# Norms of layer 1 made in layer 0, halo copies on Pool's queue, own slots for raw weights: one change to a two-layer attention and feed-forward kernel

## The chip, the cores and the metric

The kernel runs on one NeuronCore of a Trainium2 chip. The metric is device time in microseconds (us) of one execution; lower is better. A core has a matrix engine (PE, with its weight loads shown apart as PEld), a vector engine (DVE), an activation engine (ACT), a general one (POOL) and a sequencer that mostly issues transfers (SP). Each works through its own instructions in a fixed order, and waits on semaphores for the others. Transfers (DMA) are issued by SP, ACT or POOL and carried by 16 DMA engines that they share. In the profile an issue by such a queue is written SPq, ACTq or POOLq.

## The reference, cut to what matters

Two layers with the same weights, over 2048 tokens of width 576:

```python
x = x + _A_ref(_layernorm(x), A_wqkv, A_wo)     # layer 0
x = x + _B_ref(_layernorm(x), B_w1, B_w2)
x = x + _A_ref(_layernorm(x), A_wqkv, A_wo)     # layer 1
x = x + _B_ref(_layernorm(x), B_w1, B_w2)
# _A_ref: 32 heads of 18; each token attends to 8 tokens: itself and those 2, 4, .. 14 before it
# _B_ref: silu(x @ w1) @ w2, hidden width 4608
# _layernorm: (x - mean) / sqrt(var + 1e-5), no gain and no bias
```

## The kernel before

**Tiling.** The tokens are cut into 4 chunks of 512 (4 tiles of 128 tokens, index `j`). With two layers there are 8 stages, `s` = 0 to 7; stage `s` is layer `s // 4`, chunk `s % 4`. Each stage has a norm, the query-key-value product (QKV), the attention, the projection (`project`), a second norm, and the feed-forward part (`ffn`). All products run in f16 pairs: an operand is split into a high and a low half, and a product is the sum of three matmuls. From stage 3 on the first product of `ffn` is made by a scheme with seven products in place of eight (`pair_z`, L1051), whose weights `prepare` makes on DVE, ACT and POOL during layer 0.

**QKV and attention.** Heads are worked in 4 units `u` of 8 heads. For stage 0 and for layer 1 PE makes a unit's QKV for 4 tiles (`qkv_matmul`, L693, 14 matmuls of 432 columns for a tile), and ACT copies keys and values to a tile `kv` (L759) and queries to `qt` (L761). There are two `kv` tiles. A token's older neighbours lie on another partition, so four small transfers copy them within `kv` (`halo`, L771): ACT's queue issues them. Only then can DVE multiply queries by keys (L790, 128x2304 f32), sum (L794), make the softmax, weigh the values (L823) and sum them (L830, L831). For stages 1 to 3 of layer 0 the QKV products are made early, during stage 0, while the raw QKV weights are at hand (`qkv_ahead`; ACT evacuates at L706 and SP stores to DRAM).

**First `ffn`.** During stage 0's `ffn` the weights `w1` and `w2` arrive raw in f32 (`raw_load`, L896 to L900, POOL's queue). ACT sums their squares (L917, L919), PE adds across partitions (L922), DVE makes a power of two (`pow2`), ACT and DVE split into halves (L931 to L938), and POOL's queue stores the halves for later stages (L941, L943). Raw tiles and halves share 8 slots `w1` and 10 slots `w2`.

**Norms.** `layer_norm` takes mean and variance on DVE (L466, L467), an inverse root by three Newton steps of four small DVE instructions each (L490 to L496), then normalizes and splits, on ACT and DVE or on DVE alone, and transposes either on PE (first norm and the stage 0 ones) or by a DMA transpose of SP's queue (L442). Layer 1's first norms are made at the head of stages 4 to 7, on DVE alone (L545, L550, L425).

**What sets the order.** The program is written as operations with a planned engine, duration, priority, reads and writes. A list scheduler (`Plan.order`) plays them through and writes each engine's instructions in the order it finds, lower `prio` first among those ready. `after=` binds the planned order only. On the chip an instruction waits for the data and slots that it uses and for the instructions ahead of it on its engine. So the order of every engine is fixed before the run, and a changed duration or slot moves instructions in places far from the edit.

Of the kernel before, what the change touches and what calls it, by code (L numbers as in the profile page):

```python
# [276 lines left out]
def sliding_attention_silu_ffn(ctx: ExitStack, tc: tile.TileContext, x, wqkv, wo, w1, w2, out):  # L277
# [27 lines left out]
    def cut(a):  # L305
# [49 lines left out]
    xd = [[tc.dram_tile([P, D], F32, name=f"xd{c}{j}") for j in range(NJ)] for c in range(NC)]  # L355
    w1s = [tc.dram_tile([P, 10 * P], F16, name=f"w1s{f}") for f in range(NFT)]
# [37 lines left out]
    d1 = cp.tile([P, NFT], F32, name="d1")  # L394
# [8 lines left out]
    du = cp.tile([P, NU], F32, name="du")  # L403
# [46 lines left out]
    marks = []  # L450

    def layer_norm(xs, prio, into, on_act, on_pe=False, late=()):

        st, mv, nt, xT = Buf("st"), Buf("mv"), Buf("nt"), Buf(into)
# [26 lines left out]
        def newton():  # L481
            v, r, a, b = (T(nt)[:, i, :] for i in (0, 1, 3, 4))
# [6 lines left out]
            for i in range(3):  # L489
                nc.vector.tensor_tensor(a, r, r, op=ALU.mult)  # L490
                nc.vector.tensor_tensor(a, a, v, op=ALU.mult)
                nc.vector.tensor_scalar(b, a, -0.5, 1.5, op0=ALU.mult, op1=ALU.add)
                if i < 2:
                    nc.vector.tensor_tensor(r, r, b, op=ALU.mult)
                else:
                    nc.vector.scalar_tensor_tensor(r, r, LNS, b, op0=ALU.mult, op1=ALU.mult)  # L496
            if on_act == 1:
                nc.vector.tensor_scalar(T(nt)[:, 2, :], T(mv)[:, :, 0], -1.0, None, op0=ALU.mult)
        op("DVE", 2.6, newton, [(st, j) for j in range(NJ)] + [(mv, j) for j in range(NJ) if on_act < 2], [nt], prio)
        if into == "xt":  # L500
            for j in range(2):
# [30 lines left out]
                op("ACT", 2.6, hi, [(ys, 0), (ys, 1)], [(yh, 0)], prio)  # L532
# [7 lines left out]
            return xT  # L540
        for j in range(NJ):
# [10 lines left out]
            if on_act:  # L552
                op("ACT", 0.74, lambda j=j, y=y: nc.scalar.activation(T(y), T(xs[j]), AF.Identity,
                                                                      bias=T(nt)[:, 2, j:j + 1]),
                   [xs[j], nt], [y, (xT, "hold")], prio)
# [31 lines left out]
    def raw_wq(u):  # L587
# [4 lines left out]
        for k in range(5):  # L592
            def load(k=k):
                d = raw(k).rearrange("p (t c) -> p t c", t=3)
                for p0, n, row in ((0, P, k * P),) if k < 4 else ((0, 64, 512), (64, 64, 512)):
                    nc.sync.dma_start(d[p0:p0 + n], wqkv[row:row + n, :].rearrange(
# [4 lines left out]
            op("SP", 0.8 if k < 4 else 1.3, load, [], [rs[k]], WQ[u], nbytes=P * 3 * UC * 4, after=gate[3:4] if u > 1 else ())  # L601
# [6 lines left out]
        def scale():  # L608
# [36 lines left out]
    def raw_wo():  # L645
# [17 lines left out]
        def scale():  # L663
# [6 lines left out]
            nc.vector.tensor_scalar(DO, so[:, 3:4], ru[:, NU:], 1.0 / HSH, op0=ALU.mult, op1=ALU.mult)  # L670
# [19 lines left out]
    def qkv_matmul(xT, w, j, m):  # L690
        pl = list(passes(lambda k: T(xT)[:, k, j * P:(j + 1) * P], w))
# [543 lines left out]
```

## Time and profile before

| | before |
|---|---|
| runs shown | 2209.05, 2196.72, 2195.46 us; median 2196.72 us |
| profiled execution, its own time | 2203.91 us |
| its span, first to last instruction | 2202.1 us |
| PE busy | 2127.9 us, 97% |
| DVE busy | 1649.3 us, 75% |
| ACT busy | 932.9 us, 42% |
| POOL busy | 403.4 us, 18% |

The profiled execution is one run under the hardware profiler; its time is 7.2 us above the median of the runs shown. Shares are means over the whole span, and the stages differ: stage 0 up to its projection lasts to about 195 us, the first `ffn` to about 487 us, layer 1 starts near 975 us. A view by stage says more than the mean. A row of the timeline gives start, duration, engine, line, operation, tiles and count, and in brackets the engine's idle time before it with what ended the wait.

### The profile page before, as it was taken

What the parts mean: (1) busy time and instruction counts of PE and PEld (TensorE: products, weight loads), DVE (VectorE), ACT (ScalarE), POOL (GpSimd) and SP (SyncE); (2) the same over time, 40 slices, a digit from 0 to 9 for tenths busy, and PEclk for the clock granted to TensorE, in tenths of its full rate; (3) what the DMA queues carried; (4) which work ended last, traced back from release to release, by engine and by line L of the source; (5) the groups of instructions that cost most, each with busy time, mean ns of one, the idle gap of its engine ahead of it and who ended that gap; (6) DMA issues with size and microseconds to landing.
All of it is one profiled execution on the core that took longest, in us unless ns stands there. A gap on an engine that the chain in (4) does not pass through costs nothing.

```text
span 2202.1 us, 39553 instructions
## 1 busy us (share of the span) xinstructions
PE 2127.9 (97%) x15676; PEld 1532.1 (70%) x15676; DVE 1649.3 (75%) x2658; ACT 932.9 (42%) x1649; POOL 403.4 (18%) x617
## 2 busy tenths in 40 slices
PE   6799998999999999999999999999999999999999
PEld 3346555666756566577788767887778877888887
DVE  7889899999999985457885479855997559873322
ACT  7245667644243533333432433334443333433332
POOL 2124345421356554400001000000000000000000
PEclk9899999999999999999999999999999999999999
DMA  7777566885787777675556845676655964567542
GB/s 194 147 197 267 182 227 213 206 283 204 198 257 236 242 193 205 206 205 175 174 167 168 242 129 160 176 206 187 194 153 140 263 186 142 162 150 221 156 137 74
DMA packets 295201, 419.64 MB, mean 191 GB/s; under 512 B 150040, under 2 KB 181636, under 8 KB 291048
## 3 DMA queue, kind: packets, MB, share of 16 engines
q1 hardware_dynamic: 249344, 274.91, 45.0%
q0 software_dynamic: 35936, 98.79, 14.1%
q10 hardware_dynamic: 9736, 43.42, 6.2%
q8 instruction: 122, 2.00, 0.4%
q14 instruction: 63, 0.52, 0.1%
HBM read 298.47 MB, written 67.68 MB: 166 GB/s over the span
## 4 chain that ended last, share of the span: by engine, by line
PE 73%; issue 11%; DVE 8%; DMA 6%; ACT 1%; POOL 1%; ACTq 0%; SPq 0%; DVEq 0%; POOLq 0%
PE acc L1137 30%; PE z L1051 17%; PE z L1124 12%; PE z L693 10%; PE acc L862 4%; DMA w<-in_B_w_dram 1%; DVE pr L823 1%; DMA rb<-yh 1%; DVE pr L830 1%; DVE pr L790 1%; DVE lg L794 1%; DVE x L869 1%; DMA qd<-hs 1%; DMA w<-w2s 1%; DVE w L933 1%
## 5 line engine op out<-in xcount | busy, mean ns | idle before, releaser
L1137 PE MATMUL acc<-w,h 128*128 128x288 f16 x6912 | 883.8, 286 | 2.4 <-DVE x L869 2.4
L1137 PEld LDWEIGHTS <-h 128*128 128x128 f16 x6912 | 676.1, 98 | 175.8 <-issue 3.4
L1051 PE MATMUL z<-rb,w 128*128 128x256 f16 (+1 forms) x4410 | 522.5, 273 | 8.5 <-ACT hs L1056 7.5
L1051 PEld LDWEIGHTS <-w 128*128 128x128 f16 (+1 forms) x4410 | 430.1, 98 | 76.4 <-issue 10.5
L1124 PE MATMUL z<-rb,w 128*128 128x512 f16 x1512 | 335.7, 382 | 12.1 <-ACT hs L1126 5.3
L693 PEld LDWEIGHTS <-rb 128*128 128x128 f16 x1792 | 177.3, 99 | 170.9 <-issue 17.2
L869 DVE SCALAR_TENSOR_TENSOR x<-acc,d,x 128x576 f32<-128x576 f32 x192 | 156.2, 815 | 178.3 <-PE acc L1137 177.1
L1124 PEld LDWEIGHTS <-w 128*128 128x128 f16 x1512 | 148.5, 99 | 187.5 <-issue 5.4
L1031 ACT ACTIVATE h<-hs,sh 128x512 f16<-128x512 f32 x288 | 200.6, 717 | 159.4 <-PE acc L1137 146.9
L1033 DVE SCALAR_TENSOR_TENSOR h<-hs,sh,h 128x512 f16<-128x512 f32 x288 | 207.2, 746 | 69.9 <-ACT h L1031 69.1
L693 PE MATMUL z<-ra,rb 128*128 128x432 f16 x1176 | 231.0, 353 | 16.8 <-DMA rb<-yh 14.7
L1056 ACT ACTIVATE hs<-z 128x256 f32<-128x256 f32 x270 | 98.0, 379 | 331.8 <-PE z L1051 295.8
L1059 DVE TENSOR_TENSOR hs<-z,hs 128x256 f32<-128x256 f32 x270 | 109.8, 418 | 164.7 <-PE z L1051 83.5
L790 DVE TENSOR_TENSOR pr<-qt,kv 128x2304 f32<-128x2304 f32 x64 | 163.3, 2552 | 16.2 <-DMA kv<-kv 10.6
L823 DVE TENSOR_TENSOR pr<-kv,pe 128x1152 f32<-128x1152 f32 x128 | 169.8, 1351 | 0.8
L794 DVE TENSOR_REDUCE lg<-pr 128x128 f32<-128x2304 f32 x64 | 163.0, 2547 | 0.8
L1151 POOL DMA_DIRECT2D out_dram<-x x16 | 8.7, 543 | 835.2 <-DVE x L869 825.5
L1063 ACT ACTIVATE hs<-hs,dt 128x256 f32<-128x256 f32 (+1 forms) x180 | 109.3, 612 | 85.3 <-DVE hs L1059 85.1
L1126 ACT ACTIVATE hs<-z,d 128x512 f32<-128x512 f32 x108 | 73.9, 685 | 168.5 <-PE z L1124 165.0
L830 DVE TENSOR_TENSOR pr<-pr 128x1152 f32<-128x1152 f32 (+1 forms) x128 | 135.1, 1056 | 3.2
L862 PE MATMUL acc<-wo,oT 128*128 128x288 f16 x896 | 115.4, 289 | 5.6 <-DVE x L869 2.7
L862 PEld LDWEIGHTS <-oT 128*128 128x128 f16 x896 | 88.1, 99 | 30.0 <-DMA oT<-yh 3.1
(191 smaller groups left out, 1683.8 us busy)
## 6 DMA issues: line engine op xcount, KB each, us to landing
w<-wts SPq DMA_DIRECT2D x270, 320.0 KB
w<-w2s SPq DMA_DIRECT2D x252, 288.0 KB
w<-w1s SPq DMA_DIRECT2D x72, 320.0 KB
kv<-kd ACTq DMA_DIRECT2D x12, 1584.0 KB
ra<-wqs SPq DMA_DIRECT2D x17, 1080.0 KB
w<-wts SPq DMA_DIRECT2D x90, 160.0 KB
w1s<-w POOLq DMA_DIRECT2D x36, 320.0 KB, 3.2
w<-in_B_w_dram POOLq DMA_DIRECT2D x36, 288.0 KB, 4.8
```

Of the source, the lines that this page charges most:

```text
L693: nc.tensor.matmul(T(m)[:, :3 * UC], a, b, start=n == 0, stop=n == len(pl) - 1)
L790: nc.vector.tensor_tensor(T(pr), T(qt)[:, j:j + 2, None, :].to_broadcast([P, 2, W, UC]), win(T(kv), j, 2), op=ALU.mult)
L794: nc.vector.tensor_reduce(T(lg)[:, j:j + 2].rearrange("p a w h -> p (a w h)"), T(pr).rearrange("p a w (h d) -> p (a w h) d", d=DH), axis=A ...
L823: nc.vector.tensor_tensor(T(pr)[:, a].rearrange("p w (h d) -> p w h d", d=DH), v, T(pe)[:, j + a, :, :, None].to_broadcast([P, W, UH, DH]) ...
L830: nc.vector.tensor_tensor(t[:, :, 0:h, :], t[:, :, 0:h, :], t[:, :, h:2 * h, :], op=ALU.add)
L862: nc.tensor.matmul(T(acc)[:, h, 0:288], a, b[:, h * 288:(h + 1) * 288], start=n == 0, stop=n == len(pl) - 1)
L869: nc.vector.scalar_tensor_tensor(t, T(acc)[:, :, 0:288], d, t, op0=ALU.mult, op1=ALU.add)
L1031: op("ACT", 0.72, lambda: nc.scalar.activation(T(h)[:, 0, :], T(hs), AF.Copy, scale=sh[:, f:f + 1]), [(hs, 0), (hs, 1), key], [(h, 0)], pd)
L1033: op("DVE", 0.75, lambda: nc.vector.scalar_tensor_tensor(T(h)[:, 1, :], T(hs), sh[:, f:f + 1], T(h)[:, 0, :], op0=ALU.mult, op1=ALU.subtract),
L1051: nc.tensor.matmul(T(z)[:, 0:HT], T(w[m // 2])[0:q, 2 * j + m % 2 if m < 6 else j, :], T(xT)[0:q, 5 * c + i, :], start=first and n == 0, s ...
L1124: nc.tensor.matmul(T(z), v, u, start=m == 0, stop=m == len(pl) - 1)
L1137: nc.tensor.matmul(T(acc)[:, h, 0:288], T(hb[q])[:, a, j * P:(j + 1) * P], T(wbs[q][0])[:, w, h * 288:(h + 1) * 288], start=q == 0 and m = ...
```

## The change

1. **First norms of layer 1.** At the end of `ffn` of stages 0 to 3 a `layer_norm` with `ahead_of=s` normalizes the finished chunk (ACT and DVE), transposes by SP into an `oT` slot and stores to DRAM (`xls`, POOL's queue). Stages 4 to 7 load it (`load_xl`, SP) where they made the norm.
2. **Halos** are issued by POOL's queue. Stages 1 to 3 fetch `kv` and `qt` by SP's queue where ACT's did.
3. **Raw weights** from tile `RAW0` = 4 on have slots of their own, six `r1` and four `r2`, cut from the areas `ra` and `rb` that hold QKV weights and normed chunks until stage 0's QKV is done.
4. **Shorter root.** Two steps of four instructions in place of three; constant factors are folded into other places, which drops one small DVE instruction in each weight split (`d1`, `du`).
5. **Stage 0's start.** The raw QKV weights of unit 0 come by ACT's queue beside the chunk on SP's. The first norm writes its high half in one ACT instruction in place of two, with one more on DVE (`on_act == 3`); the second chunk's norm uses ACT as well.
6. **QKV ahead.** The products of chunk 2 are listed after all units of chunks 0 and 1.
7. The second norm of stage 1 stays on ACT; loads that were held back by the last transposes are held by the ACT splits before them (`held`).

```diff
+        ("r1", [(r, o + 10 * P * i, o + 10 * P * (i + 1)) for r, o in (("ra", 0), ("rb", 3 * XW)) for i in range(3)], cut(10), True),
+        ("r2", [(2 * XW + 2 * D * i, 2 * XW + 2 * D * (i + 1)) for i in range(4)], cut(2), True),
...
-            for i in range(3):
-                nc.vector.tensor_tensor(a, r, r, op=ALU.mult)
+            for f, g in ((1.0, 1.0), (9.0 / 64 * ROOT, ROOT)):
+                nc.vector.scalar_tensor_tensor(a, r, f, r, op0=ALU.mult, op1=ALU.mult)
                 nc.vector.tensor_tensor(a, a, v, op=ALU.mult)
-                nc.vector.tensor_scalar(b, a, -0.5, 1.5, op0=ALU.mult, op1=ALU.add)
...
+                nc.vector.scalar_tensor_tensor(a, a, 10.0 / 3 * g, a, op0=ALU.subtract, op1=ALU.mult)
+                nc.vector.scalar_tensor_tensor(r, a, 5.0 * g * g, r, op0=ALU.add, op1=ALU.mult)
...
+            if on_act == 3:
+                op("ACT", 0.78, lambda j=j, yh=yh: nc.scalar.activation(
+                    fl(T(yh))[:, 0:D], T(xs[j]), AF.Identity, scale=T(nt)[:, 1, j:j + 1], bias=T(nt)[:, 2, j:j + 1]),
+                   [xs[j], nt], [(yh, 0)] + hold, prio)
+                op("DVE", 0.6, norm, [xs[j], (mv, j), nt], [y], prio)
...
+            if ahead_of is not None:
+                t = Buf("oT")
+                transposed(yh, lambda t=t: T(t), t, j, prio)
+                op("POOL", 0.6, lambda j=j, t=t: nc.gpsimd.dma_start(xls[ahead_of][:, 9 * P * j:9 * P * (j + 1)], fl(T(t))),
+                   [(t, j)], [("xls", ahead_of, j)], prio, nbytes=P * 9 * P * 2)
...
-            op("SP", 0.8 if k < 4 else 1.3, load, [], [rs[k]], WQ[u], nbytes=P * 3 * UC * 4, after=gate[3:4] if u > 1 else ())
+            op("SP" if u else "ACT", 0.8 if k < 4 else 1.3, load, [], [rs[k]], WQ[u] - (0 if u else 20), nbytes=P * 3 * UC * 4, after=gate[3:4] if u > 1 else ())
...
-                        nc.scalar.dma_start(t[p0 + d:p0 + d + n, i:i + m], t[p0:p0 + n, 11 - m:11])
-                op("ACT", 3.2, halo, own, [(kv, "halo")], pr_ - 0.2, nbytes=P * 14 * UC * 4)
+                        nc.gpsimd.dma_start(t[p0 + d:p0 + d + n, i:i + m], t[p0:p0 + n, 11 - m:11])
+                op("POOL", 2.4, halo, own, [(kv, "halo")], pr_ - 0.2, nbytes=P * 14 * UC * 4)
...
-        a, b = raws[f] = Buf("w1"), Buf("w2")
+        a, b = raws[f] = (Buf("w1"), Buf("w2")) if f < RAW0 else (Buf("r1"), Buf("r2"))
...
-        late = marks[PACE_W[f]:PACE_W[f] + 1] if f < len(PACE_W) else ()
+        late = marks[PACE_W[f]:PACE_W[f] + 1] if f < len(PACE_W) else done[-1:]
...
-            o = attention(s, layer_norm(X[s], s - 1.0, "xl", False, late=turned[-2:]), lambda u: load_wq(u, s - 1.0))
+            o = attention(s, load_xl(s), lambda u: load_wq(u, s - 1.0))
...
+        if s < NC:
+            layer_norm(X[s], min(s + 0.6, 1.1), None, True, ahead_of=s)
```

Three places show what the scheduler made of it. In the kernel after the change the same statements stand some 13 to 15 lines lower (L771 is L785, L896 is L910, L759 is L773).

The first place is ACT's order before, in stage 0, where unit 1's keys are evacuated: the halo of unit 0's tile `kv_76` stands behind weight splits and between evacuations.

```order
L759 ACTIVATE kv_77<-z_131,du 128x288
L761 ACTIVATE qt_81<-z_131,du 128x144
L617 ACTIVATE h_116<-w_109,su 128x432
L617 ACTIVATE h_117<-w_110,su 128x432
L771 DMA kv_76<-kv_76 112x1152
L771 DMA kv_76<-kv_76 15x1152
L771 DMA kv_76<-kv_76 112x864
L771 DMA kv_76<-kv_76 14x864
L759 ACTIVATE kv_77<-z_132,du 128x288
```

After the change these four stand in POOL's order, between the loads of chunks 1 and 2 (`x_70` to `x_73`), and the store of the last rows of `kv_76`:

```order
L1175 DMA x_71<-in_A_x_dram 128x576
L785 DMA kv_76<-kv_76 112x1152
L785 DMA kv_76<-kv_76 15x1152
L785 DMA kv_76<-kv_76 112x864
L785 DMA kv_76<-kv_76 14x864
L1175 DMA x_72<-in_A_x_dram 128x576
L791 DMA kd_267<-kv_76 2x1152
```

Nothing but a load of x now stands between unit 0's evacuations and its halo; ACT issues no halo at all.

The second place is ACT's order after the change, at the end of unit 1's own QKV (`kv_77`). Each L720 evacuates a tile of a product made ahead, each L773 one of chunk 0's own.

```order
L773 ACTIVATE kv_77<-z_131,ru 128x288
L775 ACTIVATE qt_81<-z_131,ru 128x144
L720 ACTIVATE w_93<-z_129,ru 128x432
L562 ACTIVATE y_87<-x_70,nt_127 128x576
L565 ACTIVATE yh_88<-y_87,nt_127 128x576
L720 ACTIVATE w_94<-z_130,ru 128x432
L630 ACTIVATE h_113<-w_106,su 128x432
```

Here 16 products of chunk 1 follow before unit 2's own, and the two steps of chunk 2's norm (L562, L565) lie between them; before, chunk 2's products came with each unit, right after chunk 1's.

The third place is POOL's order in the first `ffn`. Before, raw loads (L896, L898) take `w` slots, one behind a store (L941) each:

```order
L941 DMA w1s_158<-w_95 128x1280
L896 DMA w_99<-in_B_w_dram 128x4x128
L898 DMA w_99<-in_B_w_dram 64x128 x2
L941 DMA w1s_159<-w_94 128x1280
L896 DMA w_100<-in_B_w_dram 128x4x128
L898 DMA w_100<-in_B_w_dram 64x128 x2
```

After, the first loads into the areas `rb` and `ra` follow one another with no store between them:

```order
L910 DMA rb<-in_B_w_dram 128x4x128
L912 DMA rb<-in_B_w_dram 64x128 x2
L914 DMA rb<-in_B_w_dram 128x576
L910 DMA ra<-in_B_w_dram 128x4x128
L912 DMA ra<-in_B_w_dram 64x128 x2
L914 DMA rb<-in_B_w_dram 128x576
L910 DMA ra<-in_B_w_dram 128x4x128
```

A raw load of the steady state no longer takes a slot that PE has to free.

More of the change, by code (lines that the diff above doesn't have):

```diff
@@ L39 @@
 SF = 3
+RAW0 = 4
 PREP = 1.2
@@ L45 @@
 LNS = 512.0
+ROOT = (LNS * 9 / 64) ** 0.5
 HSH = 2.0 ** -5
@@ L355, in sliding_attention_silu_ffn @@
     xd = [[tc.dram_tile([P, D], F32, name=f"xd{c}{j}") for j in range(NJ)] for c in range(NC)]
+    xls = [tc.dram_tile([P, 9 * TB], F16, name=f"xls{c}") for c in range(NC)]
     w1s = [tc.dram_tile([P, 10 * P], F16, name=f"w1s{f}") for f in range(NFT)]
@@ L449, in sliding_attention_silu_ffn, with layer_norm @@
     turned, scaled, read = [], [], []
-    marks = []
-    def layer_norm(xs, prio, into, on_act, on_pe=False, late=()):
-        st, mv, nt, xT = Buf("st"), Buf("mv"), Buf("nt"), Buf(into)
+    marks, done, held = [], [], []
+    def layer_norm(xs, prio, into, on_act, on_pe=False, ahead_of=None):
+        st, mv, nt, xT = Buf("st"), Buf("mv"), Buf("nt"), Buf("oT" if ahead_of is not None else into)
         view = lambda: T(xT)
@@ L481, in newton @@
         def newton():
-            v, r, a, b = (T(nt)[:, i, :] for i in (0, 1, 3, 4))
+            v, r, a = (T(nt)[:, i, :] for i in (0, 1, 3))
             if on_act == 2:
@@ L531, in layer_norm @@
                 op("DVE", 1.9, sums, [(ys, 0)], [(ys, 1)], prio)
-                op("ACT", 2.6, hi, [(ys, 0), (ys, 1)], [(yh, 0)], prio)
+                held.append(op("ACT", 2.6, hi, [(ys, 0), (ys, 1)], [(yh, 0), (xT, "hold", j)], prio))
                 op("DVE", 2.5, lo, [(ys, 0), (ys, 1), (yh, 0)], [(yh, 1)], prio)
@@ L540, in layer_norm @@
             return xT
+        hold = [(xT, "hold")] if ahead_of is None else []
         for j in range(NJ):
@@ L560, in layer_norm @@
             else:
-                op("DVE", 0.6, norm, [xs[j], (mv, j), nt], [y, (xT, "hold")], prio,
-                   after=late)
+                op("DVE", 0.6, norm, [xs[j], (mv, j), nt], [y] + hold, prio)
                 o = op("DVE", 1.2, halves, [y], [(yh, 0), (yh, 1)], prio)
+            gate.append(o)
+            if ahead_of is not None:
[3 more added lines that the diff above has]
+                   [(t, j)], [("xls", ahead_of, j)], prio, nbytes=P * 9 * P * 2)
+                continue
             transposed(yh, lambda j=j: T(xT)[:, :, j * P:(j + 1) * P], xT, j, prio, on_pe)
-            gate.append(o)
         return xT
@@ L638, in load_wq @@
         op("SP", 0.4, lambda: nc.sync.dma_start(fl(T(w.bufs[0])), wqs[u]), [("wqs", u)], w.keys, prio, nbytes=P * 20 * QR,
-           after=turned[-2:] + preps[TARDY - 6:TARDY])
+           after=held[-2:] + preps[TARDY - 6:TARDY])
         return w
@@ L926, in scale @@
             pow2(T(m)[:, 0:2 * n], fl(s12[:, sl, :]), fl(r12[:, sl, :]), 2 * n)
-            nc.vector.tensor_scalar(d1[:, sl], r12[:, sl, 0], 1.0 / LNS, None, op0=ALU.mult)
-        op("DVE", 0.75, scale, [m], [("s12", f) for f in fs], prio)
+        op("DVE", 0.6, scale, [m], [("s12", f) for f in fs], prio)
         for f, (wa, wb) in zip(fs, wab):
@@ L961, in fn @@
         def fn():
-            for o, q, f, t in ((ALU.min, s12, 0.25, st1), (ALU.max, r12, 4.0 / LNS, dt1)):
+            for o, q, f, t in ((ALU.min, s12, 0.25, st1), (ALU.max, r12, 4.0, dt1)):
                 nc.vector.tensor_reduce(t, q.rearrange("p (g a) t -> p g t a", a=2)[:, :, 0, :], axis=AX.X, op=o)
@@ L1167, in load_x, with load_xl @@
         return xs
+    def load_xl(s):
+        xT = Buf("xl")
+        op("SP", 0.4, lambda: nc.sync.dma_start(T(xT).rearrange("p j a b -> p (j a b)"), xls[s - NC]),
+           [("xls", s - NC, j) for j in range(NJ)], [(xT, j) for j in range(NJ)], s - 1.0, nbytes=P * 9 * TB * 2,
+           after=held[-2:] + preps[TARDY - 6:TARDY])
+        return xT
     X, XT, ahead = {}, {}, []
@@ L1180, in more @@
                 qkv_ahead(1, u, x1, w)
-                qkv_ahead(2, u, x2, w)
                 ahead.append((u, w))
             o = attention(0, xT, raw_wq, more)
+            for u, w in ahead:
+                qkv_ahead(2, u, x2, w)
             x3 = layer_norm(load_x(3, -1.2, gate[11:12]), -1.2, "xa", True, PE_LN[3])
```

51 lines of the change are left out of this document (24 added, 27 removed).

## The prediction, made before the changed kernel ran

> **What bounds the kernel now.** I read the page first, then the stages, then the waits inside the stages that lose time.
>
> ```profile
> span 2202.1 us, 39553 instructions
> PE 2127.9 (97%) x15676; PEld 1532.1 (70%) x15676; DVE 1649.3 (75%) x2658; ACT 932.9 (42%) x1649; POOL 403.4 (18%) x617
> PE   6799998999999999999999999999999999999999
> ```
>
> PE is busy 97% of the span, and the change takes no matmul away: 15676 before and after. So only PE's idle time and its slow clock can be won, and the row of slices puts them at the start. The view by stage gives amounts: stage, its length, busy time of PE, PEld, DVE, ACT and POOL, then the granted clock.
>
> ```profile
> 58.00:195.00 137.00, 117.45 (x624) 61.67 (x624) 119.84 (x147) 51.68 (x98) 32.80 (x44) 0.93 0.70 177
> 237.00:400.00 163.00, 148.86 (x932) 91.84 (x931) 149.18 (x211) 109.19 (x191) 76.75 (x134) 0.97 0.67 218
> 400.00:778.00 378.00, 377.25 (x2443) 238.52 (x2441) 363.75 (x572) 169.31 (x233) 153.21 (x226) 1.00 0.77 230
> 778.00:950.00 172.00, 168.16 (x1103) 108.29 (x1101) 98.04 (x203) 57.65 (x72) 84.55 (x119) 0.99 0.72 198
> 950.00:1250.00 300.00, 298.56 (x2418) 235.54 (x2416) 215.62 (x357) 120.90 (x236) 12.12 (x17) 1.00 0.66 189
> 1250.00:1300.00 50.00, 44.53 (x322) 32.49 (x321) 29.34 (x32) 14.62 (x30) 1.87 (x3) 0.93 0.57 165
> ```
>
> PE's idle time is length less busy time: 19.6 us in 58 to 195 (stage 0's attention), 14.1 in 237 to 400 (the first `ffn`), 0.8 in 400 to 778, 3.8 in 778 to 950, 5.5 in 1250 to 1300. In the first of these DVE is the engine to look at: it is busy 119.8 of 137 us, and the projection that ends the stage waits for it. Where PE is full, a faster DVE or ACT brings nothing.
>
> **Term A, stage 0 up to its projection.** In the timeline:
>
> ```profile
> 37.31 0.37 ACT L761 ACTIVATE qt<-z,du 128x144 f32<-128x144 f32 x1
> 47.41 0.62 ACTq L771 DMA_DIRECT2D kv<-kv  x1
> 55.74 4.98 ACTq L771 DMA_DIRECT2D kv<-kv  x3
> 57.25 2.55 DVE L790 TENSOR_TENSOR pr<-qt,kv 128x2304 f32<-128x2304 f32 x1
> 70.03 4.81 PE L693 MATMUL z<-ra,rb 128*128 128x432 f16 x14 [12.45 <-DMA rb<-yh]
> 157.13 18.05 PE L693 MATMUL z<-h,rb 128*128 128x432 f16 x98 [0.58 <-ACT w L706]
> 187.57 0.46 DVE L831 TENSOR_TENSOR o<-pr 128x288 f32<-128x288 f32 x1
> 195.35 7.04 PE L862 MATMUL acc<-wo,oT 128*128 128x288 f16 x56 [1.15 <-ACT oT L440]
> ...
> DVE yh L425 <- ACT yh L556: 11.7, 5, 4.6
> ```
>
> Unit 0 is evacuated at 37.68, but its halo is issued by ACT only at 47.41, and DVE's first product starts at 57.25, 9.8 us after that issue. On POOL only a load of x stands ahead of the halo, so the 9.7 us go. The evacuation itself comes earlier: the first norm loses one ACT instruction a tile and four Newton instructions.
>
> ```profile
> L553 ACT ACTIVATE y<-x,nt 128x576 f32<-128x576 f32 x16 | 12.3, 771 | 11.7 <-DVE yh L425 11.5 <-DVE nt L498 0.2
> L490 DVE TENSOR_TENSOR nt<-nt 128x4 f32<-128x4 f32 x48 | 7.8, 162 | 1.6
> L466 DVE BATCH_NORM_STATS2 st<-x 128x6 f32<-128x288 f32 x128 | 51.7, 446 | 8.8 <-DMA x<-xd 5.5 <-DMA x<-in_A_x_dram 2.4
> L467 DVE BATCH_NORM_AGGREGATE mv<-st 128x2 f32<-128x12 f32 x64 | 13.4, 209 | 2.2
> L425 DVE SCALAR_TENSOR_TENSOR yh<-y,nt,yh 128x512 f16<-128x512 f32 x16 | 11.9, 742 | 12.7 <-ACT yh L556 11.7 <-DMA kv<-kv 0.9
> L425 DVE SCALAR_TENSOR_TENSOR yh<-y,nt,yh 128x64 f16<-128x64 f32 x16 | 4.5, 278 | 0.0
> L620 DVE SCALAR_TENSOR_TENSOR h<-w,su,h 128x432 f16<-128x432 f32 x5 | 3.1, 661 | 0.0
> ```
>
> That is 4 x 0.771 + 4 x 0.162 = 3.7 us at most; other ACT work stands between, so I take 3 (0 to 4). First product: 57.25 - 9.7 - 3 = 44.5, or 12.7 us earlier. Against it, the new DVE order moves work of before behind the first product: two tiles' statistics (4 x 0.404 busy + 2 x 0.209 = 2.0), a root of 11 small instructions (1.8), five splits (3.3), a low half (1.0): 8.1 us. DVE's idle time in this stage is 17.2 us; 11.7 us of its waits up to 195 are low halves that wait for ACT's high halves, and ACT stood in a halo issue for 4.98 us at 55.74 or waited for transposes. ACT is now free of halos, but the transposes still share the DMA engines with them. I take half of the idle time as gone, 8.6 (0 to 17.2).
>
> DVE's last sum then ends at 188.0 - 12.7 + 8.1 - 8.6 = 174.8, and the projection, 7.3 us behind it as before (195.35 less 188.03), starts at 182, 13.2 us earlier. By PE's new order 57 groups of 14 matmuls stand ahead of it where 55 stood; at 18.05 / 7 = 2.58 us that is 5.2 us of work less to do behind it. PE's own 57 groups are 147 us, less than 182 by more than the start takes, so PE now waits at the projection for DVE rather than at 70.03 for a transpose. After a wait the clock is low: the 14 matmuls at 70.03 took 4.81 us, 2.2 more than 2.58. I charge that: **A = -13.2 - 5.2 + 2.2 = -16**, from -5 (evacuation as before, idle time stays) to -27 (all idle time goes).
>
> **Term B, the first `ffn`.**
>
> ```profile
> 286.09 0.76 POOL L896 DMA_DIRECT2D w<-in_B_w_dram  x1 [5.09 <-PE z L1124]
> 287.86 0.68 ACT L919 ACTIVATE junk<-w 128x576 f16<-128x576 f32 x1 [4.29 <-DMA w<-in_B_w_dram]
> 293.25 4.60 PE L1124 MATMUL z<-rb,w 128*128 128x512 f16 x14 [4.22 <-ACT hs L1126]
> 297.83 3.18 PE L1124 MATMUL z<-rb,w 128*128 128x512 f16 x14
> ...
> ACT junk L917 <- DMA w<-in_B_w_dram: 12.4, 4, 5.9
> ACT junk L919 <- DMA w<-in_B_w_dram: 8.7, 5, 4.3
> ```
>
> This is one chain: the raw load waits for PE to free a slot, ACT's sum of squares waits for the raw tile, and behind it in ACT's order stands the evacuation that PE waits for. ACT lost 12.4 + 8.7 = 21.1 us so in this stage. Own slots cut the first link. PE's idle time is 14.1 us, and two long waits cost 1.4 us each of clock (4.60 against 3.18). DVE's and ACT's other work still comes between, so I take 8 idle and 2 clock: **B = -10**, from 0 to -17. The instructions dropped from each split and root are counted at nothing here: DVE's order around them moves by more than they last.
>
> **Term C, ACT's block in layer 1.**
>
> ```profile
> 1278.28 5.92 SPq L879 DMA_DIRECT2D w<-w2s  x6
> 1279.68 10.94 ACTq L771 DMA_DIRECT2D kv<-kv  x4
> 1291.10 3.15 PE L1051 MATMUL z<-rb,w 128*128 128x256 f16 x14 [5.46 <-ACT hs L1056]
> ```
>
> The four halo issues held ACT for 10.9 us while SP issued weights, and PE stood 5.46 us for an evacuation. Issued by POOL, which is busy 1.87 of 50 us there, they hold nothing: **C = -6** with some clock, from 0 to -7.
>
> **Edits at nothing.** Layer 1's DVE loses four norms, but PE is busy 298.6 of 300 us beside them. The work that they add to layer 0 is, for a chunk, 8 x 0.404 + 4 x 0.209 of statistics, 12 x 0.162 of root and 4 x (0.742 + 0.278) of low halves: 10 us, and three chunks of it fall due before stage 3's projection: 30 us. What hides it is PE's order: 84 matmuls of L1124 and 180 of L1137 more stand ahead of that projection.
>
> ```profile
> 590.32 17.80 PE L1137 MATMUL acc<-w,h 128*128 128x288 f16 x144
> 607.96 18.29 PE L1124 MATMUL z<-rb,w 128*128 128x512 f16 x84
> ```
>
> At 18.29 / 84 and 17.80 / 144 that is 40 us, ahead of stage 1's projection (84 and 108) 32 us. DVE also idled 14.3 us in 400 to 778. Without this cover the price is the 30 us. The stores of normed chunks (POOL), the 16 transposes and the loads (SP) are the transposes of before plus 1.2 MB each way, at some 200 GB/s 12 us of transfer time beside full PE. The 3.8 us around 790, where PE waits for DVE and its buffers, I leave as they are (+-4).
>
> **Sum.** -16 - 10 - 6 = -32. The profiled execution took 2203.9 us (span 2202.1 and 1.8 around it), so 2171.9; the median of the runs shown is 7.2 us lower, and the forecast stands on it: 2196.7 - 32 = **2165**. Its own range is 2148 to 2180.
>
> **Rivals.**
>
> *Stage 0 stays with DVE (0.15).* The idle time of DVE in 58 to 195 stays, and A is -5; ACT's waits go only in part, B -6; C -6. That gives 2196.7 - 17 = 2180. For it: DVE is 87% busy there, and chunk 2's halves still wait for transposes. Against it: the late halo issue is a plain queue effect.
>
> *The raw loop starves PE (0.08, the slower side).* With four `r2` slots the load of pair n+2 waits until pair n is split. The loop is: issue of a pair, landing, squares, split, and a DVE or ACT turn behind attention.
>
> ```profile
> w<-in_B_w_dram POOLq DMA_DIRECT2D x36, 288.0 KB, 4.8
> ```
>
> Issue about 5 us (0.76 for L896, three more of some 0.54, twice), landing 4.8, four sums of squares at 0.68 or more 3, the split 5 (an estimate from the same row: as many elements, on ACT and then on DVE), two turns of 2.55: 23 us, against two pairs on PE of 28 x 0.218 + 48 x 0.124 = 12 each, 24. From 24 us on it decides: there are some 8 such double pairs, and if each load takes the 5.9 us longer that ACT waited at worst, plus 2 us of cold clock, the loss is 8 x (4.9 + 2) = 55, the result 2196.7 - 22 + 55 = 2230.
>
> *POOL's issues are blocked by DVE (0.07).* A halo's four issues could each wait for a DVE instruction: 4 x 2.55 = 10.2 us before the first product, later ones being hidden by the second `kv` tile. That gives 2165 + 10 = 2175.
>
> ```profile
> 63.75 2.55 DVE L790 TENSOR_TENSOR pr<-qt,kv 128x2304 f32<-128x2304 f32 x1
> 64.98 0.54 POOL L1162 DMA_DIRECT2D x<-in_A_x_dram  x1 [2.11 <-ACT y L553]
> ```
>
> Against it: a POOL issue took 0.54 us inside such a product, as it does elsewhere. The Trainium skill, page "SBUF — State Buffer", section "SBUF: two separate sides", states this rule: a DVE instruction in a two-port mode holds a port that GpSimd needs to write descriptors, and a transfer issued from there stands still until it ends, where one from ACT's or SP's queue would not. By that rule the change moves the halos to the wrong queue; by these rows it costs nothing here.
>
> *DVE is overfull in layer 0 (0.05).* The 30 us of norms are not hidden: 2195.
>
> **How the numbers follow.** The forecast has 0.65. About 1% is what a measurement of this kernel can tell from no change, so below 2174.7 is faster. The forecast gives 0.58 of that and 0.07 of same; the blocked issues and DVE's stage 0 give 0.09 of faster between them and 0.13 of same; overfull DVE 0.05 of same; the starved loop is slower, 0.08. Together 0.67, 0.25 and 0.08. The range reaches over the forecast and most of the first and third rival, 2142 to 2190; left out are the starved loop, most of the overfull DVE and the best ends of all terms together.
>
> **What would show it.** Halo issues on POOL with none on ACT; the first L790 (then L804) near 44; the first projection near 182, with a PE wait of some 10 us ahead of it; ACT's waits for raw tiles in the first `ffn` a few us in place of 21.1; no ACT block in layer 1. The prediction is wrong if the first product is late behind a load of x in POOL's order, if the projections of stages 1 to 3 show long waits for DVE, or if ACT still waits for raw weights.

## The result, and the profile after

The changed kernel took 2171.75 us (median of 4 runs, 2170.76 to 2174.24) beside 2197.43 us for the kernel before, a ratio of 0.9874, 95% interval [0.9844, 0.9904]. Run again with the last experiments it took 2172.75 us, a ratio of 0.9882 [0.9862, 0.9902]. That is 1.2% faster; the forecast of 2165 is 7 us low, and the measured time lies inside its range. The profiled execution took 2170.76 us, 33.1 us less than that of before. Of e10's six executions one took 3133.81 us at a mean granted clock of 0.668, and e10's ratio leaves that one out.

The page of the changed kernel, in the lines that were shown of before:

```profile
span 2169.0 us, 39537 instructions
PE 2116.9 (98%) x15676; PEld 1529.5 (71%) x15676; DVE 1623.5 (75%) x2541; ACT 958.4 (44%) x1685; POOL 455.3 (21%) x713
PE   5999899999999999999999999999999999999998
```

The stages follow, in the same stretches (stage, length, busy PE, PEld, DVE, ACT, POOL, then the granted clock):

```profile
58.00:195.00 137.00, 134.40 (x789) 75.36 (x787) 133.79 (x176) 69.20 (x127) 41.57 (x60) 1.00 0.75 223
195.00:237.00 42.00, 29.27 (x164) 16.03 (x163) 40.12 (x67) 17.48 (x29) 17.89 (x30) 0.80 0.59 193
237.00:400.00 163.00, 162.76 (x1035) 100.70 (x1034) 140.19 (x211) 130.16 (x235) 90.12 (x158) 1.00 0.70 236
778.00:950.00 172.00, 170.63 (x1170) 114.22 (x1169) 115.64 (x247) 71.14 (x102) 92.73 (x132) 1.00 0.85 233
1250.00:1300.00 50.00, 50.00 (x393) 38.18 (x392) 47.49 (x54) 22.78 (x43) 7.09 (x12) 1.00 0.58 175
```

PE's idle time fell from 19.6 to 2.6 us in stage 0's attention, from 14.1 to 0.2 in the first `ffn`, from 3.8 to 1.4 at 778, and from 5.5 to 0 at 1250. One stretch went the other way: 195 to 237 now has 12.7 us of idle and a clock of 0.80. Of before the same stretch reads:

```profile
195.00:237.00 42.00, 40.65 (x299) 27.01 (x300) 40.27 (x85) 29.11 (x52) 16.78 (x29) 1.00 0.78 271
```

The timeline after, around the steps of the prediction (start, length, engine, line, matmuls; in brackets the idle time before it and what ended it):

```profile
25.41 3.57 PE L707 MATMUL z<-ra,rb 128*128 128x432 f16 x14
48.44 2.56 DVE L804 TENSOR_TENSOR pr<-qt,kv 128x2304 f32<-128x2304 f32 x1 [1.35 <-DMA kv<-kv]
71.16 9.11 PE L707 MATMUL z<-wo,rb 128*128 128x432 f16 x49
172.96 0.46 DVE L845 TENSOR_TENSOR o<-pr 128x288 f32<-128x288 f32 x1
178.29 7.02 PE L876 MATMUL acc<-wo,oT 128*128 128x288 f16 x56
205.47 0.16 DVE L496 SCALAR_TENSOR_TENSOR nt<-nt 128x4 f32<-128x4 f32 x1
205.55 2.62 DVE L837 TENSOR_TENSOR pr<-kv,pe 128x1152 f32<-128x1152 f32 x2
213.43 0.57 DVE L548 TENSOR_SCALAR y<-x,mv,nt 128x576 f32<-128x576 f32 x1
214.55 0.40 PE L441 MATMUL acc<-ident,yh 128*128 128x128 f16 x4 [1.82 <-DVE yh L553]
218.95 0.61 PE L441 MATMUL acc<-ident,yh 128*128 128x128 f16 x4 [3.09 <-DVE yh L553]
223.34 0.61 PE L441 MATMUL acc<-ident,yh 128*128 128x128 f16 x4 [2.81 <-DVE yh L553]
```

The 12.45 us wait for a transpose at 70 is gone, and the projection starts at 178.29 instead of 195.35. But behind it comes stage 0's second norm. DVE finishes its root at 205.6, then does 7.8 us of stage 1's attention, and only at 213.43 makes the first normed tile; PE waits for this tile and the next two. The first `ffn` starts at 230.87, where it was 236.85: of 17.1 us gained at the projection, 6.0 are left.

At the end of the program something else is new. Both kernels end in a drain of POOL's queue (count, shortest/median/longest ns); the first row is of before, the second of after:

```profile
L1231 POOLq DRAIN  x3: 40/102/3291, 2198.1 to 2201.9; - x3
L1255 POOLq DRAIN  x3: 46/98/8229, 2159.9 to 2168.6; - x3
```

For the sums below I use **lost time**: the length of a stretch less what its matmuls take at steady pace (the median distance between two like matmuls in the trace after: 0.182 us with 432 columns, 0.216 with 512, 0.122 with 288, 0.109 with 256, 0.082 for a transpose). It holds PE's idle time and its slow clock together; small negative numbers are the error of the steady pace. The stretch 1300 to 2150 alone holds some 7000 matmuls, so 0.001 us of pace moves its column by 7 us in every row alike: compare rows, and do not read a late column by itself. The profiled executions, in us, with the start of the first `ffn` (e12, the changed kernel again, gives the row of after within 0.6 us in every column):

```
stretch           0-30 30-185 185-230 230-400 400-700 700-1000 1000-1300 1300-2150  end | first ffn
before            21.8   27.7     0.3    20.7     1.9      6.8       8.0       0.2  5.3 | 236.85
after             24.2    4.1    15.6     4.9     0.7      2.1      -0.4      -2.1 10.4 | 230.87
e1 halos on ACT   25.0    4.4    12.0     4.0     5.7      8.4       2.1       2.3  5.7 | 224.97
e2 raw shared     24.6    4.6    13.2    23.4     9.6      4.2       4.0      -3.0  9.7 | 227.11
e3 norms back     24.4    4.1    15.5     5.3     4.1      4.6       7.2      -0.4  9.2 | 231.27
e4 weights on SP  20.8    6.5    14.7     1.4     0.6      2.3       0.0      -2.6 10.3 | 226.69
e5 c2 in turn     25.7   26.9    -1.0    11.0     4.9      1.4       0.3      -3.2 10.4 | 237.73
e6 before + raw   21.8   26.5     1.1    16.5     6.1      2.9       7.9       2.1  5.3 | 235.36
e7 no hold        25.1    4.6     9.7     2.3     0.5      4.5       0.9      -3.0  9.9 | 223.22
e8 e4 + e7        20.6    5.5     9.5     2.4     0.5     11.3       0.5      -2.6 10.0 | 220.24
e9 before + c2    21.8   15.1     7.4    21.7    23.5      5.0       8.0       1.7  5.1 | 232.44
e10 before+three  21.8    3.3    16.6     2.3     0.6      2.6       7.5       2.3  9.5 | 226.00
e11 three better  20.1    5.8    11.1     2.3     0.5      9.2       3.1      -2.6  9.9 | 220.65
```

From before to after: +2.4 at the start, -23.6 in stage 0, +15.3 at the second norm, -15.8 in the first `ffn`, -5.9 in 400 to 1000, -8.4 in 1000 to 1300, -2.3 behind it, +5.1 at the end: -33.2, which is the difference of the two profiled executions.

### The profile page after: what moved, and what is told of

Same layout as the page of the kernel before. It is cut to its first block, busy times and chain, and to the rows that moved or that the text cites. A ratio compares the mean times of both kernels' runs of the same rounds, so it can differ in the third digit from the quotient of the medians.

```text
span 2169.0 us, 39537 instructions
## 1 busy us (share of the span) xinstructions
PE 2116.9 (98%) x15676; PEld 1529.5 (71%) x15676; DVE 1623.5 (75%) x2541; ACT 958.4 (44%) x1685; POOL 455.3 (21%) x713
## 4 chain that ended last, share of the span: by engine, by line
PE 65%; issue 18%; DVE 8%; DMA 5%; ACT 1%; POOL 1%; SPq 0%; ACTq 0%; POOLq 0%; DVEq 0%
PE acc L1150 28%; PE z L1064 14%; PE z L1137 13%; PE z L707 7%; PE acc L876 3%; DMA rb<-in_B_w_dram 1%; DVE lg L808 1%; DVE pr L837 1%; DMA w<-in_B_w_dram 1%; DVE pr L844 1%; DMA w<-wts 1%; DVE pr L804 1%; DVE yh L428 1%; DMA w<-in_A_wqkv_dram 0%; DVE st L469 0%
## 5 line engine op out<-in xcount | busy, mean ns | idle before, releaser
L707 PE MATMUL z<-ra,rb 128*128 128x432 f16 x1176 | 224.8, 347 | 2.3 <-ACT qt L775 2.2
L1139 ACT ACTIVATE hs<-z,r 128x512 f32<-128x512 f32 x108 | 73.9, 685 | 167.1 <-PE z L1137 166.4
L773 ACT ACTIVATE kv<-z,ru 128x288 f32<-128x288 f32 x80 | 39.6, 495 | 156.1 <-PE z L707 156.1
```

Source lines behind the costliest of these rows:

```text
L707: nc.tensor.matmul(T(m)[:, :3 * UC], a, b, start=n == 0, stop=n == len(pl) - 1)
```

## The experiments

All are timed in five rounds against the kernel before. One thing holds for each of them: the planner makes a new order of the whole program out of every edit, so a kernel with one edit undone differs from its neighbour in more than that edit.

**e1: halos back on ACT.**

```diff
-                nc.gpsimd.dma_start(t[p0 + d:p0 + d + n, i:i + m], t[p0:p0 + n, 11 - m:11])
-        op("POOL", 2.4, halo, own, [(kv, "halo")], pr_ - 0.2, ...)
+                nc.scalar.dma_start(t[p0 + d:p0 + d + n, i:i + m], t[p0:p0 + n, 11 - m:11])
+        op("ACT", 3.2, halo, own, [(kv, "halo")], pr_ - 0.2, ...)
```

> The changed kernel with one edit undone: the neighbours' keys (halos) are issued by ACT again, all else as changed. Theory: the block of ACT in layer 1 comes back (four halo issues of ACT beside SP's weight loads held it for 10.94 us before, and PE stood 5.46 us near 1291), and the first product of stage 0 is a few us later than 48.4: 2171.8 + 5 to 6 for layer 1 + 0 to 8 in stage 0 = 2177 to 2186, with a PE gap of about 5 us near 1280 to 1290. Rival (the block went because the transposes and loads at stage 4's head were reordered when the norms left it, and the queue is not what matters): 2170 to 2174, no PE gap there.

2180.05 us, ratio 0.9906 [0.9893, 0.9919]: slower than the changed kernel, in the theory's range. ACT's block returned; here are ACT's queue, SP's queue and PE, near 945 and not at 1280 to 1290 where the 5 us were expected (there four issues took 5.94 us and PE waited 1.91):

```profile
944.86 8.39 ACTq L785 DMA_DIRECT2D kv<-kv  x4
948.77 6.87 SPq L445 DMA_TRANSPOSE oT<-yh  x1
954.82 3.45 PE L1064 MATMUL z<-rb,w 128*128 128x256 f16 x17 [4.01 <-ACT hs L1069]
```

The bound on layer 1 was right (8.8 us more lost from 700 to 1300 than after). In stage 0 the reading was wrong:

```profile
60.85 2.55 DVE L804 TENSOR_TENSOR pr<-qt,kv 128x2304 f32<-128x2304 f32 x1
187.02 3.23 PE L876 MATMUL acc<-wo,oT 128*128 128x288 f16 x25
```

DVE's first product came 12.4 us later than with halos on POOL, and PE lost only 0.3 us more for it in 30 to 185: the projection starts 8.7 us later, but 60 products stand ahead of it instead of 57, which is 7.7 us of work, and the first `ffn` starts earlier, at 224.97. The end is 4.7 us shorter, since POOL's drain is 3.54 us.

**e2: raw weights in the slots of the split ones.**

```diff
-RAW0 = 4
+RAW0 = 99
-        late = marks[...] if f < len(PACE_W) else done[-1:]
+        late = marks[...] if f < len(PACE_W) else ()
```

> The changed kernel with one edit undone: all raw weights of the first ffn go through the slots of the split weights again, with no hold on the projections ahead, all else as changed. Theory: ACT's waits for raw tiles return (21.1 us before, 7.0 now in 223 to 400) and with them PE's idle time of that stage (14.1 us before and its cold clock, 0.2 now): 2171.8 + 10 to 17 = 2182 to 2189. Rival (ACT free of halos, or the other order of DVE, ended these waits): 2169 to 2175.

2201.7 us, ratio 1.0009 [0.9996, 1.0021]. The theory's sign, about twice its size: the whole gain is gone. In the first `ffn` (waits of ACT: total, times, longest):

```profile
ACT junk L931 <- DMA w<-in_B_w_dram: 22.7, 6, 6.0
ACT junk L933 <- DMA w<-in_B_w_dram: 7.1, 2, 5.7
368.15 0.59 PE L936 MATMUL z<-accw,ones 128*128 128x4 f32 x2 [4.22 <-ACT junk L933]
```

ACT waits 29.8 us for raw tiles, and the lost time rises by 18.5 us in 230 to 400, by 8.9 in 400 to 700 and by 4.4 in 1000 to 1300.

**e3: layer 1's norms at the head of its stages.**

```diff
-        if s < NC:
-            layer_norm(X[s], min(s + 0.6, 1.1), None, True, ahead_of=s)
...
-            o = attention(s, load_xl(s), lambda u: load_wq(u, s - 1.0))
+            o = attention(s, layer_norm(X[s], s - 1.0, "xl", False), lambda u: load_wq(u, s - 1.0))
```

The layout of the tile `xl` goes back with it.

> The changed kernel with one edit undone: layer 1's first norms are made at the head of stages 4 to 7 again, nothing of them is kept in memory, all else as changed. Theory (the moved norms cost and bring nothing, PE being full on both sides): 2171.8 +- 3, PE idle under 4 us in 1250 to 1300. First rival (layer 1 waited for these norms): slower by the 5.5 us of PE idle before at 1250 to 1300, 2175 to 2179. Second rival (their 10 us of DVE a chunk are paid in layer 0): faster, 2160 to 2168, with less PE idle time before 400.

2184.69 us, ratio 0.9932 [0.992, 0.9944], above all three answers' ranges. So the moved norms are worth about 12 us beside the other edits. The lost time grew most between 900 and 1250; the longest waits there are for DMAs:

```profile
937.60 2.59 PE L1064 MATMUL z<-rb,w 128*128 128x256 f16 x22 [2.78 <-DMA w<-wts]
1188.35 1.91 PE L1064 MATMUL z<-rb,w 128*128 128x256 f16 x14 [1.31 <-DMA rb<-o]
1192.88 2.39 PE L1064 MATMUL z<-rb,w 128*128 128x256 f16 x9 [2.62 <-DMA rb<-o]
```

Both expected causes fail: none of these waits is for a first norm (`wts` are packed weights, `rb<-o` the transposes of a second norm), and the time lost before 400 did not change. Nor do the transposes of the first norms stand in the way here: SP issued no transpose between 900 and 945, and ahead of the second norm's transposes SP's queue stood 7.2 us for DVE's low halves (L531). That norm is late itself: its stage's projection starts at 1142.2, where it starts at 1101.8 after the change. How the norm at the head makes the planned stage later is not shown.

**e4: unit 0's raw weights on SP.**

```diff
-                    (nc.sync if u else nc.scalar).dma_start(...)
-            op("SP" if u else "ACT", ..., WQ[u] - (0 if u else 20), ...)
+                    nc.sync.dma_start(...)
+            op("SP", ..., WQ[u], ...)
```

> The changed kernel with one edit undone: unit 0's raw weights are issued by SP behind x again, not by ACT beside it, all else as changed. Theory: the start is about 4 us earlier (x of chunk 0 lands by 7 in place of 9.4, the first QKV product begins near 21 in place of 25.4), stage 0's projection follows by as much, and the second norm behind it gives part of it back: 2166 to 2171. Rival (the projection and the first ffn are paced by DVE's sum of work, not by the start): 2171 to 2174, with the first ffn at 230 to 232 as now.

2165.17 us, ratio 0.9842 [0.9829, 0.9855]: the theory, just below its range. In the changed kernel these loads run beside those of x, and ACT takes sums of squares of unit 1's weights, which it must wait for, ahead of the first norm's high halves:

```profile
13.35 0.56 ACT L614 ACTIVATE junk<-w 128x432 f16<-128x432 f32 x1 [1.14 <-DMA w<-in_A_wqkv_dram]
15.42 0.56 ACT L614 ACTIVATE junk<-w 128x432 f16<-128x432 f32 x1 [1.42 <-DMA w<-in_A_wqkv_dram]
16.94 1.61 ACT L556 ACTIVATE yh<-x,nt 128x576 f16<-128x576 f32 x2
```

With SP the first QKV product starts 4.5 us earlier:

```profile
20.95 6.22 PE L707 MATMUL z<-ra,rb 128*128 128x432 f16 x23
```

The first `ffn` starts 4.2 us earlier, so the start counts nearly in full. Two steps of the theory fail: the projection did not follow (179.81, with 58 products ahead in place of 57), and the second norm gave nothing back. Of the 6.6 us won, the rest lies behind the start: 3.5 us less are lost in 230 to 400.

**e5: chunk 2's products with each unit.**

```diff
                 qkv_ahead(1, u, x1, w)
+                qkv_ahead(2, u, x2, w)
                 ahead.append((u, w))
-            for u, w in ahead:
-                qkv_ahead(2, u, x2, w)
```

> The changed kernel with one edit undone: chunk 2's products ahead are put in with each unit of chunk 0 and 1 again, not behind all units. Theory: PE's idle time in 30 to 185 (23.6 us more before than after the change) went because PE no longer meets chunk 2's products, whose normed tiles come late by DMA, among those of chunks 0 and 1; the early halos did not do it, since with halos on ACT the first product of stage 0 came at 60.85 and PE still lost only 4.4 us there. So a wait of about 12 us for a transposed tile near 70 comes back, and the first ffn begins 10 to 20 us later than 230.87: 2172 + 10 to 18 = 2182 to 2190. Rival (norm 1 made on ACT, not the place of chunk 2's products, or the early start of DVE ended that wait): 2170 to 2174, no PE wait above 3 us in 60 to 80.

2188.05 us, ratio 0.995 [0.9931, 0.9969], inside the theory's range. The wait returned in parts, of which these are the longest:

```profile
64.31 2.73 PE L707 MATMUL z<-ra,rb 128*128 128x432 f16 x14 [1.97 <-DMA rb<-yh]
70.50 4.41 PE L707 MATMUL z<-ra,rb 128*128 128x432 f16 x14 [3.46 <-DMA rb<-yh]
76.19 2.73 PE L707 MATMUL z<-ra,rb 128*128 128x432 f16 x14 [1.28 <-DMA rb<-yh]
```

Lost time in 30 to 185 is 26.9 us, as before the change (27.7), with the halos on POOL. In this stage the gain hangs on the place of chunk 2's products. The account behind it holds in part: of PE's 18.8 us of idle time there, 7.8 are waits for transposed tiles and the rest mostly for ACT, and the first `ffn` starts only 6.9 us later, not 10 to 20, since the 15.6 us lost at the second norm fall to nothing. Another 6.1 us are lost in 230 to 400.

**e6: the kernel before with own slots for raw weights** (the slots `r1` and `r2`, and the edit of e2 the other way round).

> The kernel before with one edit made: the raw weights of the first ffn from the fifth tile on in slots of their own, held until the last product ahead; all else as before. Theory (the own slots are worth what the waits of the first ffn were, whatever else is changed): 2199 - 10 to 17 = 2182 to 2189. Rival (undone in the changed kernel they cost 29.7 us, so they are worth that): 2167 to 2173. Second rival (their worth shows only with ACT free of halos): 2194 to 2200.

2199.83 us, ratio 0.9994 [0.998, 1.0007]: the second rival's number; theory and first rival fall. ACT's waits for raw tiles did shrink, from 21.1 to 8.2 us, but PE still lost 16.5 us in 230 to 400, and 4.2 more in 400 to 700 at stage 1's projection:

```profile
ACT junk L920 <- DMA rb<-in_B_w_dram: 5.1, 2, 3.9
ACT junk L922 <- DMA rb<-in_B_w_dram: 3.1, 2, 1.9
ACT w L934 <- DVE s L414: 8.1, 4, 3.1
408.69 3.60 PE L865 MATMUL acc<-wo,oT 128*128 128x288 f16 x28 [3.47 <-DMA oT<-yh]
```

What did not shrink is ACT's wait for DVE's scale (L414; 8.7 us before) and PE's wait for split weights (L934 on ACT, L936 on DVE): 7.5 us in 230 to 400, where it was 6.6. The partner that the second rival names, ACT free of halos, is not shown by this: no halo is issued in the first `ffn`, and e1, with halos on ACT, lost only 4.0 us there.

**e7: no hold ahead of stage 0's second norm.**

```diff
-        hold = [(xT, "hold")] if ahead_of is None else []
+        hold = [(xT, "hold")] if ahead_of is None and into != "x0" else []
```

> The changed kernel with one dependency of the planner taken from stage 0's second norm: its first DVE instruction no longer waits until the tile of the transposed result is free (that tile's last readers are products ahead on PE); the copy into it still waits. Theory: PE's waits for L553 and L428 in 212 to 230 (about 9 us and 2 to 4 us of low clock behind them) come from that hold, since DVE did 7.9 us of stage 1's attention between the root at 205.5 and the first normed tile at 213.4: the norm stands right behind the root, the waits go, 2172 - 8 to 13 = 2159 to 2164. Rival (the sum of DVE's work paces this place, so that another wait takes over, for the split weights of the first ffn or for stage 1): 2169 to 2174.

2166.53 us, ratio 0.9845 [0.9823, 0.9867]: 5 to 6 us less than the changed kernel, between the ranges of theory and rival. The norm stands right behind the root:

```profile
206.94 0.16 DVE L496 SCALAR_TENSOR_TENSOR nt<-nt 128x4 f32<-128x4 f32 x1
207.14 0.66 DVE L548 TENSOR_SCALAR y<-x,mv,nt 128x576 f32<-128x576 f32 x1
217.09 0.40 PE L441 MATMUL acc<-ident,yh 128*128 128x128 f16 x4 [1.89 <-DVE yh L553]
```

The first `ffn` starts 7.65 us earlier. What is left (9.7 us in 185 to 230) is mostly waits for the last two tiles, which DVE halves between steps of stage 1's attention (at 216.55 and 219.84), and the low clock after them.

**e8: e4 and e7 together.**

> Both of the edits that may beat the changed kernel: unit 0's raw weights on SP's queue behind x (2165.2 alone) and no hold before stage 0's second norm. Theory: they lie in different places and add up: 2165 - 8 to 12 = 2153 to 2158. Rival (either one uses up the same slack): 2160 to 2166.

2169.42 us, ratio 0.9859 [0.9838, 0.9881], above both. Up to the first `ffn` (220.24) they nearly add up, 10.6 us of 11.8; 9.2 of them are lost again in 700 to 1000, at the seam of the layers, where the two longest waits are:

```profile
920.95 4.00 PE L1064 MATMUL z<-rb,w 128*128 128x256 f16 x35 [1.69 <-DVE hs L1072]
973.09 3.46 PE L707 MATMUL z<-ra,rb 128*128 128x432 f16 x11 [2.70 <-ACT qt L775]
```

**e9: the kernel before with chunk 2's products behind all units** (the edit of e5, the other way round).

> The kernel before with one edit made: chunk 2's products ahead stand behind all units of stage 0; all else as before. Theory (the place of these products is what PE's 14.7 us of waits at 70 to 77 hang on, whatever else is changed): no PE wait above 4 us in 60 to 80, the first ffn 10 to 14 us before 236.85, and 2200 - 10 to 16 = 2184 to 2190. Rival (PE then runs into stage 0's second norm or into the raw weights, which are as late as before, as with the own slots alone): the wait at 70 goes, the first ffn gains under 5 us or loses it again by 400, and the time is 2194 to 2201.

2217.95 us, ratio 1.0079 [1.0051, 1.0108]: slower than before, beyond the rival. The 12.45 us wait at 70 went, and a 4.77 us wait for ACT came near it; the first `ffn` starts 4.4 us earlier, but then the projections of stages 1 and 2 wait for their transposes, three times and 14.6 us in all:

```profile
73.83 6.41 PE L693 MATMUL z<-wo,rb 128*128 128x432 f16 x25 [4.77 <-ACT w L706]
415.10 5.35 PE L862 MATMUL acc<-wo,oT 128*128 128x288 f16 x28 [6.40 <-DMA oT<-yh]
604.64 1.62 PE L862 MATMUL acc<-wo,oT 128*128 128x288 f16 x6 [5.13 <-DMA oT<-yh]
```

**e10: the kernel before with three edits**: chunk 2's products, own raw slots, halos on POOL (those of e9 and e6, and that of e1 the other way round).

> The kernel before with three edits made together: chunk 2's products behind all units, the raw weights' own slots, and halos issued by POOL; the norms of layer 1 stay at the head of its stages, the root, the fetches and unit 0's weights as before. Theory (these three hold the gain but each needs the others): within the 12.6 us that the moved norms are worth and a few us of the rest, so 2172 + 4 to 13 = 2176 to 2185. Rival (they bring little without the norms made on ACT and the shorter root, since DVE is as full as before in stage 0 and the first ffn): 2188 to 2200.

2179.04 us, ratio 0.9908 [0.9886, 0.993], as the theory had it. The three alone bring the early stages where the whole change brings them (3.3 us lost in 30 to 185, 2.3 in 230 to 400, 16.6 at the second norm). In the first `ffn` PE is busy throughout, while ACT waits 14.7 us for raw tiles:

```profile
237.00:400.00 163.00, 163.00 (x1043) 101.69 (x1042) 145.23 (x229) 130.22 (x234) 89.24 (x156) 1.00 0.69 233
ACT junk L922 <- DMA rb<-in_B_w_dram: 8.8, 3, 4.9
```

So ACT's waits for raw tiles are not by themselves PE's idle time. Nor do the early stages need the halos on POOL: e1 lost as little there (4.4, 4.0, and 12.0 at the second norm) with halos on ACT, beside the other edits. What is missing against the changed kernel is mostly in 1000 to 1300 (7.5 us lost), at the place that e3 showed: no halo is on ACT, and PE waits for `rb<-o` between 1150 and 1200.

**e11: e8, and the kept norms at their own chunk's priority** (`s + 0.6` in place of `min(s + 0.6, 1.1)`). **e12: the changed kernel** in the same rounds.

> The changed kernel with three edits: unit 0's raw weights on SP behind x, no hold ahead of stage 0's second norm, and the norms kept for layer 1 made at the priority of their own chunk (s + 0.6 in place of at most 1.1). Theory: the first two together lost 10 us at 900 to 1000 (PE waits for DVE and ACT at 921 to 973) that neither lost alone, because DVE took the norm of chunk 3 ahead of what stage 4's head needs; at its own chunk's priority that norm stands behind, the 10 us go and the sum of the two edits shows: 2169 - 7 to 10 = 2159 to 2162. Rival (these waits come from the start of layer 1 itself, whatever the norms' place): 2166 to 2172.

> The changed kernel as it is, on the same chip and in the same rounds as the version with three edits, so that the two are compared directly. Theory and rival alike: 2170 to 2175, a ratio of 0.987 to the kernel before.

e11 took 2171.7 us, ratio 0.9879 [0.9859, 0.9898], e12 2172.75, ratio 0.9882 [0.9862, 0.9902]: no difference. The waits at 921 to 973 did shrink, to 0.93 us at most, but 9.2 us are still lost in 700 to 1000, with a new wait at 731, and 3.1 in 1000 to 1300:

```profile
730.89 2.72 PE L1137 MATMUL z<-rb,w 128*128 128x512 f16 x6 [3.31 <-ACT hs L1139]
```

Why an earlier first `ffn` is given back between 700 and 1300 in e8 and e11, and not in e4, stays open. The fastest versions are e4 and e7 (0.9842 and 0.9845), which cannot be told apart. Only e4's interval, [0.9829, 0.9855], lies below that of e12, so e4 is the one to keep.

## Why the prediction was right in its total and wrong in its terms

**Term A** (-16; measured -5.9 up to 230). Its single steps were near: DVE's last sum ended at 173.4 (forecast 174.8), the projection started at 178.29 (182). Three steps failed. Unit 0's evacuation was to end 3 us earlier, but it ended at 39.89, 2.2 us later than before: the first QKV product started 4.65 us later, because unit 0's weights went beside x on ACT's queue (e4). So the first product stands at 48.44, not 44.5. Next, the first product was taken to pace the stage: e1 shows it 12.4 us later at no price, and e5 shows that the place of chunk 2's products paces it (alone that place gives half, 27.7 to 15.1 us lost, e9). I had that move in the order and gave it only 5.2 us, through the two more products ahead. Last and costliest, the gain was read at the projection. What stands ahead of the first `ffn` is 64 products in every one of these kernels, and the second norm behind the projection had no price: 15.3 us more were lost there. The PE wait of some 10 us that I put ahead of the projection did not come: PE's own products ended as the projection began. PE waited some 36 to 45 us later instead, for this norm (1.82, 3.09 and 2.81 us).

**Term B** (-10; measured -15.8, within its bounds). ACT's waits for raw tiles fell to 7.0 us as told:

```profile
ACT junk L933 <- DMA rb<-in_B_w_dram: 4.3, 4, 1.9
ACT junk L931 <- DMA ra<-in_B_w_dram: 2.7, 3, 1.4
```

That this alone is the gain is wrong: own slots are needed (30 us in e2) but bring nothing alone (e6), and in e10 PE is full although ACT still waits 14.7 us. The place of chunk 2's products is needed here too: e5, with own slots, lost 11.0 us in 230 to 400. Why, no run shows.

**Term C** (-6; measured -8.4 in 1000 to 1300). That ACT's block is cured by POOL's queue was right (e1). That this cure alone brings the gain was wrong: e10 has it and still lost 7.5 us in 1000 to 1300, at another place (between 1150 and 1200, where PE of before was idle for 0.2 us), so the 8.4 us need the moved norms as well. The low clock behind the block was undersized: of the 8.0 us lost before, 5.5 were idle time, and I gave the clock 0.5. The price at the other end was missed: the end takes 5.1 us more, nearly all of it POOL's drain.

**Edits at nothing.** That the moved norms would be hidden in layer 0 was right: 0.7 us lost in 400 to 700. That they bring nothing in layer 1 was wrong: e3 puts them at 12 us beside the other edits. The profile of before did not show it: there the time in 1000 to 1300 went to ACT's block at 1291, and it holds no wait for `rb<-o`, which cost 3.9 us in e3 and 2.0 in e10, with the block gone and the norms at the head. One figure of that paragraph is too small: 1.2 MB each way is one chunk's share; the trace after has 16 stores of 288 KB, 4.6 MB. It stood in no term.

**The sum and the base.** The terms gave -32, the profiled executions differ by 33.1. That is luck: A fell short by 10.1 us, B and C brought 8.2 us more than forecast, and -3.1 us came from places that had no term. The medians differ by 25.7. The forecast is low because I took a sum that was read in an execution of 2203.9 us from a median 7.2 us lower; from that execution's own time it would have been 2171.9, where 2171.75 was measured. The three runs behind that median were low themselves: in the later rounds the kernel before has medians of 2199.71 to 2201.1 us.

**Rivals.** The first rival had A's number (-5, measured -5.9) but not its way: DVE's idle time in 58 to 195 did not stay, it fell from 17.2 to 3.2 us, and the wait that took over is for DVE, at the second norm. The raw loop did not starve PE, and DVE was not overfull. POOL's issues were not blocked (80 halo issues: shortest, median and longest ns):

```profile
L785 POOL DMA_DIRECT2D kv<-kv x80: 512/535/583, 39.9 to 1802.8; - x80
```

No issue took longer than 0.583 us, though 73 of the 80 ran while a DVE instruction did. The Trainium skill's rule (page "SBUF — State Buffer", section "SBUF: two separate sides") that a DVE instruction in a two-port mode holds up POOL's descriptors costs nothing in these rows; no trace here shows whether any of this kernel's DVE instructions runs in such a mode, so they do not test the rule itself.

## What to carry to other kernels

Read a gain where the next fixed amount of work begins (here the first `ffn`, with the same 64 products ahead in every version), not at the step that is made faster, and price the next thing that the bound engine must wait for. Edits that each remove a wait need not add up: of three that together brought 0.9% here, one alone brought nothing and one alone cost 0.8% (the third was not run alone), so test them together before you drop one. A sum of waits read in one execution is subtracted from that execution's time.

## What the runs showed of the hardware beside that

The final drain of POOL's queue grew with the transfers that POOL had issued: 3.2 to 3.3 us with 578 of them (before, e6, e9), 3.5 with 594 (e1), 7.0 and 7.3 with 658 (e3, e10), 7.7 to 8.2 with 674 (after and the others). It stands behind the last output, so the 80 halos on that queue cost about 4.7 us at the very end (e1 against after); that the number of transfers is the cause, and not their kind, is not shown. And issues of ACT and SP took long where they ran side by side: four halo issues on ACT took 8.39 us while a transpose on SP took 6.87 to issue (e1); the four of a unit took 2.11 on POOL at 1288 after.
